# Attention inside a fused attention and MoE kernel: P x V regrouped over the steps of a head, one normalisation per head, one matmul for V's mean row, row maxima rounded once, weight jobs at fixed steps

## The chip, the cores and the metric

The kernel runs on one core of one Trainium2 chip. The metric is the device time of one execution in microseconds (us). Three runs of the kernel before took 681.57, 682.82 and 680.62 us, median 681.57. Engines are named as in the profile: PE is TensorE's matmul and PEld its weight load, DVE is VectorE, ACT is ScalarE, POOL is GpSimd, SP is SyncE.

## The reference

Two batches of eight heads, 768 positions of 64 numbers. Query and key vectors are hashed by the signs of six projections, and a query attends only to keys of its own bucket. A query without any such key attends to all keys alike: it gets the mean of V. After attention come two feed-forward parts, which the change leaves alone except for the preparation of some of their operands.

```python
mask = q_bucket[:, :, :, None] == k_bucket[:, :, None, :]
scores = scale * np.matmul(q, k.transpose(0, 1, 3, 2))
scores = np.where(mask, scores, -1000000000.0)
scores = scores - np.max(scores, axis=-1, keepdims=True)
attn = np.exp(scores)
attn = attn / (np.sum(attn, axis=-1, keepdims=True) + 1e-09)
return np.matmul(attn, v)
# _moe_ref:  h = max(x @ w1, x @ w2, x @ w3);  h @ w_out
# _moe2_ref: h = x @ w_in;  (h * clip(h + 3, 0, 6) / 6) @ w_out
```

## The kernel before, in words

Everything is written out in order, engine by engine; no scheduler moves work. The attention runs in 96 steps: 16 heads, two halves of 384 queries each, three pairs of key tiles per half. So a head has six steps, numbered here 0 to 5 within the head, and a pair of heads (which share a load of q, k and v) has twelve.

In a step s the PE does, in this order: the P x V product of step s-6 (`LAG = 6`), the tasks that a table puts into this step, the scores of step s (`scores`, four matmuls of 384 columns, lines L664), the matmuls that find the row maxima for a step ten ahead (`max_unit`, two matmuls, L614). ACT takes the exponential of the scores twice, once to float32 (`E`, L668) and once to float16 (`ph`, L671). POOL (in one step of twelve, and in half of those from 88 on, DVE) computes the rest `pl = E - ph` (L686). P x V multiplies ph and pl with V, itself split into two float16 parts: per step it takes one of the three query tiles of a half over all six key tiles, three matmuls of 65 columns each (L698, L699, L700), and two more that add the mean row of V for queries without a match (L703, L704: the flag row FL times the high and the low part of V's mean, tile VM). The 65th column is the sum of the row. All three query tiles of a half lie in one PSUM bank, tile `x`, of which there is one. When the half is done DVE normalises it (`norm`, L710, L715, L718), and the next half's first P x V matmul needs the bank back.

The PSUM pool `m` has three banks. It serves the maxima (each bank is free again when DVE has reduced it, L618), the transposes, V's scale (`vsum`, L543), V's mean (`vmean`, L596), the hash bits (`bits`, twelve matmuls before the scores of step 5 of every second head) and the weight jobs.

`max_fin` transposes a head's maxima (L634) and lets DVE make three small rows of them: the clipped maximum rounded to the matmul's type (L637), the rest of that rounding (L638), and the flag "no match" (L643). `max_out` sends the three rows by DMA to rows 96 and 97 of the tile of q (`QA`, shown as T) and to row 0 of FL. The second pair of score matmuls subtracts the two rows of the maximum, so it has 98 rows.

A weight job (`job`) loads one tile of the MoE weights (512 KB), makes float32 halves of it on ACT (L193 into a bank of `m`, L204) and, a step later, DVE (L217, L220, which free the bank), then rounds on ACT (L227) and takes the rest on POOL (L230). `tick` starts a job and moves the running ones on, once a step from step 39, with six ticks between two starts: steps 39, 45, 51, 57, 63, 69. `xhi` and `xlo` (L270 on ACT, L273 on DVE) split four tiles of the finished attention output. From step 88 the PE also computes the first MoE products (`hfill`, L307), two groups of three matmuls a step, which need the weights of the jobs. At the end of attention `xsum` (L284) on DVE and `tlo` (L294) on POOL prepare sums for the next stage.

Of the kernel before, what the change touches and what calls it, by code (L numbers as in the profile page):

```python
# [76 lines left out]
XH = (40, 49, 61, 69)  # L77
# [4 lines left out]
JS = 38  # L82
JG = 6
JT = 4
# [20 lines left out]
def body(ctx, tc, qT, kT, vP, projT, wts, consts, out):  # L105
# [56 lines left out]
    half = const.tile([128, 1], F32, name="half")  # L162
    prH = const.tile([128, 256], F32R, name="prH")
# [193 lines left out]
    def attention():  # L357
# [6 lines left out]
        VM = [ap.tile([128, 2, VW], F16, name=f"VM{i}") for i in range(2)]  # L364
# [180 lines left out]
        def vscale(p, k):  # L545
            if k == 0:
                t = st["vt", p] = ap.tile([128, 1], F32, name="vs_t")
                u = st.pop(("vu", p))
                dve.tensor_scalar(
                    out=t, in0=u[:, 0:1], scalar1=2.0 ** -100, scalar2=None, op0=ALU.max  # L550
                )
            elif k == 1:
                e = st["ve", p] = ap.tile([128, 1], F32, name="vs_e")
                dve.tensor_scalar(
                    out=e.bitcast(I32), in0=st.pop(("vt", p)).bitcast(I32), scalar1=0x7F800000,
                    scalar2=None, op0=ALU.bitwise_and,
                )
            elif k == 2:
                r = st["vr", p] = ap.tile([128, 1], F32, name="vs_r")
                dve.reciprocal(out=r, in_=st.pop(("ve", p)))  # L560
            else:
                dve.tensor_scalar(
                    out=up[:, p:p + 1], in0=st.pop(("vr", p)), scalar1=2.0 ** 14, scalar2=None,
                    op0=ALU.mult,
                )
# [24 lines left out]
        def vmean(p):  # L590
# [9 lines left out]
            m = ap.tile([1, 2, 64], F32, name="vm_m")  # L600
            act.activation(out=m, in_=o[0:1, :, 0:64], func=AF.Copy, scale=1.0 / S)
            vm = VM[p % 2][0:1]
            eng = pool if p else dve
            eng.tensor_copy(out=vm[:, :, 0:64], in_=m)
            eng.tensor_tensor(out=vm[:, :, 65:129], in0=m, in1=vm[:, :, 0:64], op=ALU.subtract)
# [24 lines left out]
        def max_fin(h, q=None):  # L630
# [5 lines left out]
            r = a2.tile([6, 2, 128], F32R, name="mr")[0:n]  # L636
            dve.tensor_scalar(out=r[:, 0, :], in0=m, scalar1=-0.5, scalar2=None, op0=ALU.max)  # L637
            dve.scalar_tensor_tensor(  # L638
                out=r[:, 1, :], in0=m, scalar=-0.5, in1=f32(r[:, 0, :]),
                op0=ALU.max, op1=ALU.subtract,  # L640
            )
# [47 lines left out]
        def pv(h, hf, q):  # L689
            p, j = divmod(h, 2)  # L690
            if q == 0:
                st["X", h, hf] = unit("x")
            o = st["X", h, hf][:, 66 * q:66 * q + 65]
# [12 lines left out]
        def norm(h, hf):  # L706
            p, j = divmod(h, 2)
            X = st.pop(("X", h, hf))[:, 0:198].rearrange("p (b d) -> p b d", b=3)
            d = a2.tile([128, 3], F32, name="xd")
# [4 lines left out]
            r = a2.tile([128, 3], F32, name="xr")  # L714
            dve.reciprocal(out=r, in_=d)  # L715
            if j == 0 and hf == 0:
                st["xo", p] = a2.tile([128, 6, 128], F32, name="xo")
            dve.tensor_tensor(  # L718
                out=st["xo", p][:, 3 * hf:3 * hf + 3, 64 * j:64 * j + 64], in0=X[:, :, 0:64],
                in1=r.unsqueeze(2).to_broadcast([128, 3, 64]), op=ALU.mult,  # L720
# [66 lines left out]
        for p in range(NP):  # L787
# [36 lines left out]
            for j in range(2):  # L824
# [4 lines left out]
                for hf in range(2):  # L829
                    at(s0 + 6 * j + 3 * hf + 2 + LAG, norm, h, hf)  # L830
# [25 lines left out]
        for s in range(NST + LAG):  # L856
            if 0 <= s - LAG < NST:
                pv(*idx(s - LAG))
# [22 lines left out]
            if s > JS:  # L881
                tick(1, JG if s < TAIL else JT, J0)
# [792 lines left out]
```

## Time and profile before

| what | before |
|---|---|
| time, median of three runs | 681.57 us (680.62 to 682.82) |
| the profiled execution | 680.07 us, of which the profile's span is 678.3 us |
| PE busy | 662.5 us, 98% of the span, 5189 matmuls |
| PEld busy | 611.0 us, 90% |
| DVE busy | 510.2 us, 75%, 978 instructions |
| ACT busy | 432.5 us, 64%, 749 instructions |
| POOL busy | 338.2 us, 50%, 280 instructions |
| granted TensorE clock over the span | 0.997 |

The attention takes roughly the first 250 us of the span. The busy shares are means over stages of quite different kinds: in the attention all five engines work at once, later the PE and its weight loads lead alone. A matmul's duration in the profile includes its way through the array, so it is longer than the time by which it holds up the next one; for that the starts of neighbouring matmuls are compared.

### The profile page before, as it was taken

The numbers are of one execution on the slowest core, as the hardware profiler recorded it, in microseconds if no ns is written. First come the engines' busy times: TensorE is split into PE (matmuls) and PEld (weight loads), VectorE is DVE, ScalarE is ACT, GpSimd is POOL, SyncE is SP. The second block draws the span as 40 slices with busy tenths as digits, with TensorE's granted clock in tenths as the row PEclk, the third lists the DMA queues.
The fourth block names the chain that finished last, engine by engine and source line by source line (L and its number), as shares of the span: only waits on it lengthen the run. The fifth ranks groups of instructions, "written<-read, shape, count | busy, mean of one in ns | idle before, by whom it ended". The sixth has DMA issues, their size and how long they took to land.

```text
span 678.3 us, 13481 instructions
## 1 busy us (share of the span) xinstructions
PE 662.5 (98%) x5189; PEld 611.0 (90%) x5189; DVE 510.2 (75%) x978; ACT 432.5 (64%) x749; POOL 338.2 (50%) x280
## 2 busy tenths in 40 slices
PE   8999999999999999999999999999999999999998
PEld 7789998888898989999999999988989898989886
DVE  6798988999985557677768778754868787877664
ACT  6578788889888525465665657776656565565520
POOL 6688888999988240654542673122233131313100
PEclk9899999999999999999999999999999999999999
DMA  6656656767441000222114322010303121211005
GB/s 192 168 150 150 172 143 159 197 167 190 101 98 65 1 2 31 65 86 68 62 63 125 126 63 93 32 63 0 125 21 104 32 95 36 89 63 62 1 0 187
DMA packets 22527, 61.80 MB, mean 91 GB/s; under 512 B 3864, under 2 KB 4952, under 8 KB 22464
## 3 DMA queue, kind: packets, MB, share of 16 engines
q1 hardware_dynamic: 22032, 60.55, 31.3%
q8 instruction: 41, 0.67, 0.4%
q10 hardware_dynamic: 432, 0.40, 0.2%
q14 instruction: 22, 0.18, 0.1%
HBM read 38.87 MB, written 3.15 MB: 62 GB/s over the span
## 4 chain that ended last, share of the span: by engine, by line
PE 63%; DVE 6%; ACT 2%; issue 1%; POOLq 0%; DVEq 0%; ACTq 0%
PE c L1210 16%; PE m L1210 11%; PE x L1538 10%; PE m L1538 9%; PE c L147 4%; PE m L307 3%; PE m L1453 2%; PE s L664 2%; PE c L1453 2%; PE x L1210 1%; PE x L698 1%; DVE xF L1161 1%; PE x L699 1%; PE x L700 1%; DVE mx L618 1%
## 5 line engine op out<-in xcount | busy, mean ns | idle before, releaser
L686 POOL TENSOR_TENSOR pl<-E,ph 128x768 f16<-128x768 f32 x85 | 152.4, 1807 | 30.7 <-ACT ph L671 17.1
L618 DVE TENSOR_REDUCE mx<-m 128x1 f32<-128x384 f32 x192 | 96.7, 546 | 13.1 <-PE m L614 12.1
L668 ACT ACTIVATE E<-s 128x768 f32<-128x768 f32 x96 | 78.0, 813 | 38.5 <-PE s L664 31.5
L671 ACT ACTIVATE ph<-s 128x768 f16<-128x768 f32 x85 | 68.9, 811 | 0.0
L698 PEld LDWEIGHTS <-ph 128*128 128x128 f16 x576 | 53.7, 97 | 16.3 <-issue 10.2
L698 PE MATMUL x<-VV,ph 128*128 128x65 f16 x576 | 64.2, 195 | 2.8 <-DVE xo L718 1.8
L699 PE MATMUL x<-VV,ph 128*128 128x65 f16 x576 | 63.8, 195 | 0.0
L700 PE MATMUL x<-VV,pl 128*128 128x65 f16 x576 | 63.3, 192 | 0.0
L664 PE MATMUL s<-QB,KB 128*128 128x384 f32 x192 | 57.0, 378 | 0.0
L614 PE MATMUL m<-T,T 76*128 76x384 f32 x192 | 54.0, 354 | 2.7 <-DVE mx L618 1.5
L699 PEld LDWEIGHTS <-ph 128*128 128x128 f16 x576 | 54.3, 98 | 0.7 <-issue 0.6
L700 PEld LDWEIGHTS <-pl 128*128 128x128 f16 x576 | 54.5, 99 | 0.0
L664 PE MATMUL s<-T,T 98*128 98x384 f32 x192 | 49.6, 339 | 0.2 <-DMA T<-mr 0.2
L1006 POOL TENSOR_TENSOR hF<-hF 128x256 f32<-128x256 f32 x8 | 6.9, 859 | 75.5 <-DVE hF L965 75.5
L614 PEld LDWEIGHTS m<-T,T 76*128 76x128 f32 x192 | 35.2, 189 | 8.3 <-DVE mx L618 5.5
L961 DVE SCALAR_TENSOR_TENSOR wy<-wy,wr 128x512 int32<-128x512 int32 x32 | 23.0, 718 | 22.0 <-ACT wr L956 22.0
L1556 DVE TENSOR_TENSOR xF<-x,xF 128x512 f32<-128x512 f32 (+1 forms) x43 | 29.4, 684 | 11.6 <-PE x L1538 11.5
L1094 POOL TENSOR_TENSOR hF<-hF 128x256 f32<-128x256 f32 x6 | 6.5, 1091 | 62.7 <-DVE hF L1048 62.7
L984 POOL TENSOR_TENSOR wl<-wy,wh 128x512 fp32r<-128x512 f32 x10 | 13.0, 1298 | 46.4 <-ACT wh L982 46.4
L664 PEld LDWEIGHTS s<-T,T 98*128 98x128 f32 x192 | 35.2, 190 | 0.5 <-DMA T<-mr 0.5
L984 POOL TENSOR_TENSOR wol<-wy,woh 128x512 fp32r<-128x512 f32 x6 | 8.4, 1393 | 50.9 <-ACT woh L982 50.9
L1556 DVE TENSOR_TENSOR xF<-m,xF 128x512 f32<-128x512 f32 (+1 forms) x42 | 28.5, 678 | 4.6 <-PE m L1538 4.6
(472 smaller groups left out, 2185.1 us busy)
## 6 DMA issues: line engine op xcount, KB each, us to landing
wraw<-in_wts_dram SPq DMA_DIRECT2D x56, 512.0 KB
xF<-in_vP_dram SPq DMA_DIRECT2D x8, 384.0 KB
KB<-kH SPq DMA_DIRECT2D x15, 192.0 KB
QB<-qL SPq DMA_DIRECT2D x15, 192.0 KB
T<-kH SPq DMA_DIRECT2D x15, 192.0 KB
T<-qH SPq DMA_DIRECT2D x15, 192.0 KB
KB<-kL SPq DMA_DIRECT2D x15, 192.0 KB
QB<-qH SPq DMA_DIRECT2D x15, 192.0 KB
```

The source lines that it names most:

```text
L614: pe.matmul(u[:, 0:HF], QA[h % NA][0:76, qt * 128:qt * 128 + 128], KA[h % NA][0:76, hsl(hf)], start=True, stop=True,)
L618: dve.tensor_reduce(out=mx[h][:, qt, hf:hf + 1], in_=u[:, 0:HF], axis=AX.X, op=ALU.max)
L664: pe.matmul(u[:, k, 0:HF], a[0:n, c], b[0:n, hsl(hf)], start=n == 128, stop=n < 128)
L668: act.activation(out=e, in_=u[:, :, 0:HF], func=AF.Exp, scale=BIG)
L671: act.activation(out=ph.rearrange("p (a b) -> p a b", a=2), in_=u[:, :, 0:HF], func=AF.Exp, scale=BIG,)
L686: eng.tensor_tensor(out=pl, in0=e, in1=ph, op=ALU.subtract)
L698: pe.matmul(o, ph[:, c], vv[:, 0:65], start=kt == 0, stop=False)
L699: pe.matmul(o, ph[:, c], vv[:, 65:130], start=False, stop=False)
L700: pe.matmul(o, pl[:, c], vv[:, 0:65], start=False, stop=False)
L1210: pe.matmul(u, l[:, s], r[i], start=first and i + j == 0, stop=i == 1 and j == 2, skip_group_check=not first,)
L1538: pe.matmul(u[:, 0:c1 - c0], (h, l, h)[k], (oh, oh, ol)[k][:, c0:c1], start=j == k == 0, stop=j == 1 and k == 2,)
L1556: dve.tensor_tensor(out=o, in0=u[:, 0:c1 - c0], in1=o, op=ALU.add)
```

## The change

Six edits, all in the attention:

- In step 0 of a head no P x V product is computed, in step 1 two are, in the others one. All six query tiles of a head share the bank `x`, and one `norm` per head, after step 5, replaces two.
- The flag goes to rows 0 and 32 of FL, the mean row's high and low part to rows 0 and 32 of VM: one matmul (L693 of the new file) where there were two. The flag is now 0.25 instead of 1, and V's scale carries the factor.
- The maximum has one rounded row instead of two, so the scores' second pair has 97 rows. The flag is made by ACT from that row (`Relu`), not by DVE. `max_out` still sends three rows.
- `vscale` needs three small DVE operations instead of four.
- Weight jobs start at steps 64, 76, 80, 84, 88 and 92, and `xhi` at 37, 49, 61, 73 instead of 40, 49, 61, 69.
- The three `tlo` at the end run on DVE instead of POOL.

```diff
-XH = (40, 49, 61, 69)
+XH = (37, 49, 61, 73)
-JS = 38
-JG = 6
-JT = 4
+JB = (64, 76, 80, 84, 88, 92)
...
-            m = ap.tile([1, 2, 64], F32, name="vm_m")
-            act.activation(out=m, in_=o[0:1, :, 0:64], func=AF.Copy, scale=1.0 / S)
+            m = ap.tile([33, 2, 64], F32, name="vm_m")
+            act.activation(out=m, in_=o[0:33, :, 0:64], func=AF.Copy, scale=1.0 / S)
...
-            r = a2.tile([6, 2, 128], F32R, name="mr")[0:n]
-            dve.tensor_scalar(out=r[:, 0, :], in0=m, scalar1=-0.5, scalar2=None, op0=ALU.max)
-            dve.scalar_tensor_tensor(
-                out=r[:, 1, :], in0=m, scalar=-0.5, in1=f32(r[:, 0, :]),
-                op0=ALU.max, op1=ALU.subtract,
-            )
+            r = a2.tile([6, 128], F32R, name="mr")[0:n]
+            dve.tensor_scalar(out=r, in0=m, scalar1=-0.5, scalar2=None, op0=ALU.max)
             g = a2.tile([6, 128], F16, name="mf")[0:n]
-            dve.tensor_scalar(out=g, in0=m, scalar1=-0.5, scalar2=None, op0=ALU.is_lt)
+            act.activation(out=g, in_=f32(r), func=AF.Relu, scale=-1.0, bias=mhalf[0:n, :])
...
-            for i in range(2):
-                copy(QA[h % NA][96 + i:97 + i, c], r[:, i, :], eng)
-            (eng or sp).dma_start(out=FL[h % 3][0:1, c], in_=g)
+            copy(QA[h % NA][96:97, c], r, eng)
+            for r in (0, 32):
+                (eng or sp).dma_start(out=FL[h % 3][r:r + 1, c], in_=g)
...
-            f, vm = FL[h % 3][:, c], VM[p % 2][:, j, :]
-            pe.matmul(o, f, vm[:, 0:65], start=False, stop=False)
-            pe.matmul(o, f, vm[:, 65:130], start=False, stop=True)
+            pe.matmul(o, FL[h % 3][:, c], VM[p % 2][:, j, :], start=False, stop=True)
...
-                for hf in range(2):
-                    at(s0 + 6 * j + 3 * hf + 2 + LAG, norm, h, hf)
+                at(s0 + 6 * j + 5 + LAG, norm, h)
...
-                po(98 + i, tlo, 0, k, pool)
+                po(98 + i, tlo, 0, k, dve)
...
-            if 0 <= s - LAG < NST:
-                pv(*idx(s - LAG))
+            for r in ((), (s - LAG - 1, s - LAG))[s % 6] if s % 6 < 2 else (s - LAG,):
+                if 0 <= r < NST:
+                    pv(*idx(r))
...
-            if s > JS:
-                tick(1, JG if s < TAIL else JT, J0)
+            tick(1, 0, J0 if s in JB else 0)
```

The order on the PE at a head's start (step 18, the first of the fourth head; s is the scores' bank, m the maxima's). Before:

```order
L703 LDWEIGHTS FL_139
L703 MATMUL x<-VM_136,FL_139 128x65
L704 LDWEIGHTS FL_139
L704 MATMUL x<-VM_136,FL_139 128x65
L664 MATMUL s<-QB,KB 128x384 x2
L664 MATMUL s<-T_94,T_89 128x384 x2
L614 MATMUL m<-T_90,T_95 128x384 x2
L543 MATMUL m<-vs_s,ones 128x1
L698 LDWEIGHTS ph
L698 MATMUL x<-VV_134,ph 128x65
```

The same place in the changed kernel, from the end of the P x V product of the step before:

```order
L693 LDWEIGHTS FL_139
L693 MATMUL x<-VM_136,FL_139 128x65
L655 MATMUL s<-QB,KB 128x384 x2
L655 MATMUL s<-T_94,T_89 128x384 x2
L609 MATMUL m<-T_91,T_96 128x384 x2
L655 MATMUL s<-QB,KB 128x384 x2
L655 MATMUL s<-T_95,T_90 128x384 x2
L609 MATMUL m<-T_91,T_96 128x384 x2
L543 MATMUL m<-vs_s,ones 128x1
L689 LDWEIGHTS ph
L689 MATMUL x<-VV_135,ph 128x65
```

The two matmuls with FL have become one, and the scores of two steps now follow each other with only the maxima between them; the P x V products of both come after.

The order on ACT from the exponentials of step 81 to those of step 83 (L568 is V's high part, `vhi`). Before:

```order
L668 ACTIVATE E<-s 128x768
L671 ACTIVATE ph<-s 128x768
L668 ACTIVATE E<-s 128x768
L671 ACTIVATE ph<-s 128x768
L568 ACTIVATE VV_134<-xF,up 128x12x64
L668 ACTIVATE E<-s 128x768
```

And in the changed kernel, where L563 is `vhi`, L192 and L203 the first two ACT operations of a weight job and L226 its rounding:

```order
L659 ACTIVATE E<-s 128x768
L662 ACTIVATE ph<-s 128x768
L226 ACTIVATE wh_110<-wy 128x512
L659 ACTIVATE E<-s 128x768
L662 ACTIVATE ph<-s 128x768
L563 ACTIVATE VV_135<-xF,up 128x12x64
L192 ACTIVATE m<-wraw 128x512
L203 ACTIVATE wr<-wraw 128x512
L659 ACTIVATE E<-s 128x768
```

Operations of two weight jobs now stand between these exponentials.

## Rows read from the trace of the kernel before

**Rows 1.** Busy time by stretch: two pairs of heads and the attention's end.
```profile
core 0: us, PE busy (x) PEld busy (x) DVE busy (x) ACT busy (x) POOL busy (x), PEclk, DMA share, GB/s
51.19:76.30 25.11, 24.99 (x346) 22.52 (x343) 21.97 (x56) 19.85 (x29) 22.28 (x14) 1.00 0.62 161
154.66:182.64 27.98, 26.36 (x352) 23.22 (x349) 26.32 (x62) 25.69 (x40) 26.59 (x17) 1.00 0.61 157
206.12:244.50 38.38, 36.91 (x499) 34.04 (x496) 23.85 (x44) 22.19 (x32) 23.02 (x15) 1.00 0.09 29
```
**Rows 2.** PE in order of time: start, duration, operation; one undisturbed step.
```profile
78.04 0.20 PE L704 MATMUL x<-VM,FL 128*128 128x65 f16 x1
78.07 0.60 PE L664 MATMUL s<-QB,KB 128*128 128x384 f32 x2
78.50 0.51 PE L664 MATMUL s<-T,T 98*128 98x384 f32 x2
78.85 0.51 PE L614 MATMUL m<-T,T 76*128 76x384 f32 x2
...
79.83 0.60 PE L664 MATMUL s<-QB,KB 128*128 128x384 f32 x2
```
**Rows 3.** Line L704 over the whole span: count, durations in ns.
```profile
L704 PEld LDWEIGHTS <-FL x96: 97/97/98, 36.9 to 244.0; 128*128 128x128 f16 x96
```
**Rows 4.** Waits of weight loads, 30 to 246 us: total us, times, longest.
```profile
PEld L698 <- DVE xo L718: 5.1, 10, 1.8
PEld m L543 <- DVE mx L618: 2.4, 3, 0.8
PEld m L614 <- DVE mx L618: 2.2, 7, 0.6
PEld m L614 <- DVE bt L513: 1.1, 1, 1.1
```
**Rows 5.** Waits of matmuls in the same stretch.
```profile
PE x L698 <- DVE xo L718: 1.8, 2, 1.5
```
**Rows 6.** PE in order of time, near the end of attention.
```profile
238.12 0.33 PE L307 MATMUL m<-xh,wl 128*128 128x384 f32 x1
239.92 0.20 PE L698 MATMUL x<-VV,ph 128*128 128x65 f16 x1 [1.47 <-DVE xo L718]
```
**Rows 7.** DVE in order of time, the same place.
```profile
237.71 0.95 DVE L284 TENSOR_TENSOR xF<-xF 128x768 f32<-128x768 f32 x1
...
239.78 3.88 DVE L284 TENSOR_TENSOR xF<-xF 128x768 f32<-128x768 f32 x2
```
**Rows 8.** POOL in order of time, the same place.
```profile
237.88 7.47 POOL L294 TENSOR_TENSOR T<-xF,T 128x768 fp32r<-128x768 f32 x3 [3.51 <-ACT T L290]
```
**Rows 9.** PE in order of time, behind the first head's maxima.
```profile
16.22 0.90 PE L614 MATMUL m<-T,T 76*128 76x384 f32 x2 [0.30 <-DVE mf L643]
...
18.82 0.41 PE L664 MATMUL s<-T,T 98*128 98x384 f32 x1 [0.18 <-DMA T<-mr]
```
**Rows 10.** ACT by line, 60 to 200 us: count, busy us, mean ns, idle before.
```profile
L568 ACT ACTIVATE VV<-xF,up 128x768 f16<-128x768 f32 x5 | 4.7, 938 | 2.0 <-DVE up L562 2.0
...
L204 ACT ACTIVATE wr<-wraw 128x512 int32<-128x512 uint32 x6 | 4.0, 674 | 0.0
L193 ACT ACTIVATE m<-wraw 128x512 f32<-128x512 f32 x6 | 3.9, 646 | 0.0
...
L601 ACT ACTIVATE vm_m<-m 1x128 f32<-1x128 f32 x5 | 1.3, 250 | 0.0
```
**Rows 11.** ACT in order of time, the step of rows 2.
```profile
79.11 0.81 ACT L668 ACTIVATE E<-s 128x768 f32<-128x768 f32 x1 [0.32 <-PE s L664]
79.82 0.81 ACT L671 ACTIVATE ph<-s 128x768 f16<-128x768 f32 x1
```
**Rows 12.** DVE in order of time, a head's maxima in step 33.
```profile
95.52 0.27 DVE L637 TENSOR_SCALAR mr<-m 6x128 fp32r<-6x128 f32 x1
```
**Rows 13.** ACT in order of time, the same step.
```profile
94.78 0.83 ACT L668 ACTIVATE E<-s 128x768 f32<-128x768 f32 x1
```

More of the change, by code (lines that the diff above doesn't have):

```diff
@@ L363, in attention @@
         VV = [ap.tile([128, KT, 2, VW], F16, name=f"VV{i}") for i in range(2)]
-        VM = [ap.tile([128, 2, VW], F16, name=f"VM{i}") for i in range(2)]
+        VM = [ap.tile([128, 2, 65], F16, name=f"VM{i}") for i in range(2)]
         FL = [ap.tile([128, S], F16, name=f"FL{i}") for i in range(3)]
@@ L388, in setup2 @@
             pool.memset(half, 0.5)
+            pool.memset(mhalf, -0.25)
             pool.memset(one16, 1.0)
@@ L549, in vscale @@
                 dve.tensor_scalar(
-                    out=t, in0=u[:, 0:1], scalar1=2.0 ** -100, scalar2=None, op0=ALU.max
+                    out=t, in0=u[:, 0:1], scalar1=2.0 ** -100, scalar2=2.0 ** -14, op0=ALU.max,
+                    op1=ALU.mult,
                 )
@@ L558, in vscale @@
             elif k == 2:
[L559 to L564, printed above, removed]
-                )
+                dve.reciprocal(out=up[:, p:p + 1], in_=st.pop(("ve", p)))
         def vhi(p):
@@ L599, in vmean @@
                     )
-            m = ap.tile([1, 2, 64], F32, name="vm_m")
-            act.activation(out=m, in_=o[0:1, :, 0:64], func=AF.Copy, scale=1.0 / S)
-            vm = VM[p % 2][0:1]
+            m = ap.tile([33, 2, 64], F32, name="vm_m")
+            act.activation(out=m, in_=o[0:33, :, 0:64], func=AF.Copy, scale=1.0 / S)
+            vm = VM[p % 2][0:33, :, 0:64]
             eng = pool if p else dve
-            eng.tensor_copy(out=vm[:, :, 0:64], in_=m)
-            eng.tensor_tensor(out=vm[:, :, 65:129], in0=m, in1=vm[:, :, 0:64], op=ALU.subtract)
+            eng.tensor_copy(out=vm, in_=m)
+            eng.tensor_tensor(out=vm[32:33], in0=m[32:33], in1=vm[32:33], op=ALU.subtract)
         mx = {}
@@ L660, in scores @@
             u = unit("s")
-            for a, b, n in ((KB[h], QB[h], 128), (KA[h % NA], QA[h % NA], 98)):
+            for a, b, n in ((KB[h], QB[h], 128), (KA[h % NA], QA[h % NA], 97)):
                 for k in range(2):
@@ L690, in pv @@
             p, j = divmod(h, 2)
-            if q == 0:
-                st["X", h, hf] = unit("x")
-            o = st["X", h, hf][:, 66 * q:66 * q + 65]
+            if hf == q == 0:
+                st["X", h] = unit("x")
+            o = st["X", h][:, 66 * (3 * hf + q):66 * (3 * hf + q) + 65]
             for kt in range(KT):
@@ L701, in pv, with norm @@
             c = slice(hf * HF + 128 * q, hf * HF + 128 * q + 128)
-            f, vm = FL[h % 3][:, c], VM[p % 2][:, j, :]
-            pe.matmul(o, f, vm[:, 0:65], start=False, stop=False)
-            pe.matmul(o, f, vm[:, 65:130], start=False, stop=True)
-        def norm(h, hf):
+            pe.matmul(o, FL[h % 3][:, c], VM[p % 2][:, j, :], start=False, stop=True)
+        def norm(h):
             p, j = divmod(h, 2)
-            X = st.pop(("X", h, hf))[:, 0:198].rearrange("p (b d) -> p b d", b=3)
-            d = a2.tile([128, 3], F32, name="xd")
+            X = st.pop(("X", h))[:, 0:396].rearrange("p (b d) -> p b d", b=6)
+            d = a2.tile([128, 6], F32, name="xd")
             dve.tensor_scalar(
@@ L713, in norm @@
             )
-            r = a2.tile([128, 3], F32, name="xr")
+            r = a2.tile([128, 6], F32, name="xr")
             dve.reciprocal(out=r, in_=d)
-            if j == 0 and hf == 0:
+            if j == 0:
                 st["xo", p] = a2.tile([128, 6, 128], F32, name="xo")
             dve.tensor_tensor(
-                out=st["xo", p][:, 3 * hf:3 * hf + 3, 64 * j:64 * j + 64], in0=X[:, :, 0:64],
-                in1=r.unsqueeze(2).to_broadcast([128, 3, 64]), op=ALU.mult,
+                out=st["xo", p][:, :, 64 * j:64 * j + 64], in0=X[:, :, 0:64],
+                in1=r.unsqueeze(2).to_broadcast([128, 6, 64]), op=ALU.mult,
             )
@@ L803, in attention @@
                 at(E1[1], vsum, 0)
-                for k in range(4):
+                for k in range(3):
                     po(E1[2][k], vscale, 0, k)
@@ L818, in attention @@
                 at(s0 + VS, vsum, p)
-                for k in range(4):
+                for k in range(3):
                     po(s0 + VC[k], vscale, p, k)
@@ L1644 @@
     projT = np.zeros((128, 8), dtype=proj.dtype)
-    projT[96:98, 6] = -1
+    projT[96, 6] = -1
     for j in range(2):
```

4 lines of the change are left out of this document (2 added, 2 removed).

## The prediction

> **What bounds the kernel now.** I read the views in this order: the share of each engine, the busy time by stretch, the PE's instructions in order of time, the waits, then ACT. The reader is to see that in the attention the PE sets the pace although four engines are nearly full. In the second pair of heads the PE is busy for 24.99 of 25.11 us, DVE for 21.97, POOL for 22.28 and ACT for 19.85 [rows 1]. A busy PE could still be a waiting one, so I compare starts. In an undisturbed step the scores start at 78.07 and the next step's at 79.83, so a step takes 1.76 us, and its matmuls follow each other without a hole: the last flag matmul is 0.03 us ahead of the scores, two score matmuls take 0.43, the next two 0.35 [rows 2]. ACT, the nearest other engine, starts its first exponential 1.04 us after the scores' start, and ends the second at 80.63, 2.56 us after it [rows 2, 11]. The bank of these scores is wanted again two steps later, at 3.52, so ACT may fall about 0.96 us behind before the PE feels it.
>
> The pair of heads from 154.66 takes 27.98 us, 2.87 more than the undisturbed one, with the PE busy for 26.36 [rows 1]. What is lost there is in the waits of the weight loads: 5.1 us for the normalisation (ten times), 2.4 for V's scale behind the maxima, 2.2 for maxima behind maxima and 1.1 for maxima behind the hash bits [rows 4]. The last three are all banks of `m` that DVE has not yet given back. So two things pay: fewer PE cycles per step, and fewer of these waits. Each is worth its full time, since the PE has no other slack.
>
> **The change part by part.** The sum is made against the profiled execution, 680.07 us with a span of 678.3; the median of the runs is 681.57, so the time I predict is 1.5 us above what the sum gives.
>
> *One flag matmul fewer.* It goes 96 times [rows 3], and holds up what follows by 0.03 us [rows 2]: 2.9 us. Its weight load is recorded as 97 ns long [rows 3], but loads overlap, or the step of rows 2 could not have twenty such pairs in its 1.76 us beside six larger matmuls. The Trainium skill, TensorE: Matmul & The Clock Gate, section on LDWEIGHTS, gives a load its number of columns divided by 1.2 as its time in ns, 107 for 128 columns. The trace agrees with that as a duration (97) and not as a distance (30); taken as a distance it would give an estimate of 10.3 us in place of 2.9.
>
> *P x V as 0, 2, 1, 1, 1, 1.* Number and size of matmuls stay. The first scores behind a P x V product cost 0.08 us more than the next (0.43 against 0.35 [rows 2]), because the small matmul ahead hides too little of the weight load. Step 0 now has its scores behind the maxima, which are as long as the scores, so this goes once per head: 16 x 0.08 = 1.3 us. No row shows that exact sequence; the bounds are 0 and 1.3, and I take 1.3.
>
> *One normalisation per head, a step without P x V behind it.* The bank `x` is next wanted after two steps' scores and maxima, about 2.2 us (0.78 + 0.35 twice [rows 2]), instead of one's. The wait in the middle of a head is gone with its `norm`. The weight loads lose 5.1 us [rows 4], the matmuls alone 1.8 [rows 5]. These are the bounds; between them lies the refilling of the array behind a wait. At the worst place the start is 1.80 us behind the last matmul, of which the row calls 1.47 idle [rows 6]. I take 4.5. That worst one is due to DVE's sums standing ahead of a half's `norm`, which no longer exists.
>
> *Weight jobs moved.* A job is a load of 512 KB on SP, two ACT operations of 0.65 and 0.67 us and a rounding, two DVE operations, one subtraction on POOL; from the first ACT to the last DVE operation it holds a bank of `m` [rows 10]. In the old places it does so where V's scale, the maxima and the bits want banks. Out of the third to fifth pair go the 2.4 us for V's scale and the 1.1 for the bits, where `xlo` also moves away from the step before the bits. I take 2.2 and 1.0, bounds 0 and 3.5. The jobs of steps 84, 88 and 92 land where ACT is busy 22.19 and DVE 23.85 of 38.38 us, and DMA is at 0.09 instead of 0.61 [rows 1], so their loads meet less traffic; I count them as nothing. They are done by step 100, and their weights are first multiplied after the last step, so `hfill` doesn't wait.
>
> The job of step 80 is not free. Its ACT operations come right behind `vhi` (0.94), with the rounding of the job of 76 one step earlier, and nothing but exponentials in the next steps to make good for it. ACT gets 0.94 + 0.65 + 0.67 = 2.3 us [rows 10], about 2.0 as neighbours overlap, some 0.6 for the rounding, and 0.5 as the flag waits for DVE: 3.1. The margin is 0.96, less 0.64 in step 0, where the scores come earlier (2.88 us instead of 3.52 after those two steps before), but steps without job give back about 0.35 each. I take 1.5 us of PE wait, bounds 0 and 3.1. The job of 64 sits in a pair where the bits follow and ACT can catch up: 0.3.
>
> *Maxima rounded once.* DVE loses two operations per head, and one of two `norm`, so the 2.2 us of maxima behind maxima [rows 4] should fall; I take 1.6, bounds 0 and 2.2. In the first head the PE waits 0.30 us for the flag and 0.18 for the row's DMA [rows 9]: 0.5 us. With `vscale`'s missing operation and the later heads of the first pair I take 0.8. ACT gets 17 flags. The nearest row is a small ACT copy of 250 ns [rows 10]: 4.3 us in all, beside the PE's work. The flag stands ahead of a step's exponentials and must wait for DVE's row: in step 33 that row ended at 95.79, an exponential had started at 94.78 [rows 12, 13], so there ACT would lose 1.3 us. In the steps of that kind the bits follow and cover it; in the other heads DVE comes earlier. The Trainium skill, ScalarE: Activation LUTs, Rules for kernel authors, wants a relu on VectorE, and its section on ACT_TABLE_LOAD prices an ACTIVATE with a bias operand at about 280 ns + 0.833 per element, an estimate of 387 ns here. The move goes against that rule. By it the flags would be 6.6 us of ACT time instead of 4.3, still beside the PE while ACT keeps its margin.
>
> *tlo on DVE.* POOL needs 7.47 us for the three, and while it works two sums of DVE take 3.88 us, against 0.95 for one before it [rows 7, 8]. DVE gets some 2.9 us and loses about 2. What waits for these tiles comes after the rest of `hfill`: 0.
>
> *Not counted.* Steps that are shorter by 0.1 us leave POOL (22.28 of 25.11 [rows 1]) and ACT less room; I set 1.0 us aside.
>
> Sum: 2.9 + 1.3 + 4.5 + 3.2 + 1.6 + 0.8 = 14.3, less 1.5 + 0.3 + 1.0 = 2.8: 11.5 us. 680.07 - 11.5 = 668.6; as a median 670. Its own range, from the bounds: at the best 14.3 + 0.6 + 0.6 + 0.3 = 15.8 or 666, at the worst about 5 us less gain or 675.
>
> **The rivals.**
> *ACT becomes the bound in many heads.* Then the flags' waits for DVE are not covered: nearly 1.3 us in about half of the heads would take 6 us more, 676. For it speaks that step 33 shows the delay, against it that the bits follow and that ACT is idle for 5.3 us of the undisturbed pair.
> *Waits only move.* If DVE and POOL, at 26.32 and 26.59 of 27.98 us [rows 1], are the real bound, the PE's savings turn into waits for them, and only the 1.3 and 0.5 us at free places stay: 680. Against it: the undisturbed steps show no wait at all.
> *The early scores starve.* In step 0 the scores come 2.88 us after those whose bank they need, and ACT frees it at 2.56 at the earliest. If ACT lags by more than 0.32 us there, each further bit is a PE wait, 16 times. From 0.72 us of wait in each head on this eats the whole 11.5; at 0.9 it costs 14.4, and the time is 684. Most exponentials start when the PE lets them, as the one shown [rows 11], so such a lag should be rare.
> *Weight loads are the pace.* If each removed load gave its 97 ns, the first term would be 9.3 us instead of 2.9: 663. The 0.03 us between starts speak against it. The rule of the Trainium skill, TensorE: Matmul & The Clock Gate, section on LDWEIGHTS, would make it this one.
>
> **How the numbers follow.** Forecast 0.72; ACT as the bound 0.12; waits only move 0.07; early scores starve 0.06; weight loads 0.03. About 2 us, 0.3%, can be told from no change. Forecast, ACT and weight loads are faster: 0.87. Waits only move is the same: 0.07. Starving is slower: 0.06. The range runs from 664.5, which leaves out the weight loads, to 677.5, which leaves out the two last sides: 0.8 or a little more is inside.
>
> **What would show it.** Right: L704's successor 96 times instead of 192 with FL; the scores of step 0 start about 1.13 us after those of step 5; the wait for `xo` gone; the waits for V's scale and for the bits gone in the third to fifth pair, which then take 24 to 24.5 us each. A PE wait for ACT or longer steps at 83 to 88 shows the job of 80. Wrong: waits of scores for `ph` in step 0 of most heads, a pair that stays above 25 us without a job in it, or waits for the normalisation in step 1.

## The result, and the profile after

The changed kernel took 675.88 us (median of five runs) against 681.57 of the kernel before in the same comparison: ratio 0.990, 95% interval 0.9865 to 0.9935. A second comparison gave 674.57 against 681.80, ratio 0.9892 (0.987 to 0.9913). The forecast of 670.0 had the direction right, and the measured time lies inside the range of 664.5 to 677.5; but of the 11.5 us of gain that the sum gave, 5.7 and 7.2 came by the medians. One of the first five runs took 792.48 us at a granted clock of 0.754; the ratio leaves it out, and as it was the profiled one, everything below is read from the profile of the second comparison: 674.57 us, span 672.8 against 678.3, granted clock 0.997 in both. The two profiled executions lie 5.5 us apart. That of the kernel before is 1.5 us under its median and that of the changed kernel at its own, so part of what the accounts below miss is the choice of executions.

Busy time by stretch in the changed kernel (us, then the busy time of PE, PEld, DVE, ACT and POOL with their instructions, granted clock, DMA share, GB/s). The second, third and seventh row answer to [rows 1].

```profile
17.39:51.35 33.96, 31.42 (x268) 26.87 (x267) 27.00 (x58) 22.18 (x34) 23.00 (x14) 0.95 0.62 156
...
51.35:76.25 24.90, 24.63 (x329) 22.09 (x329) 20.61 (x45) 20.23 (x30) 21.63 (x15) 1.00 0.62 154
150.86:177.24 26.38, 25.52 (x336) 22.78 (x335) 23.54 (x48) 22.89 (x36) 21.50 (x15) 1.00 0.57 153
...
101.10:177.24 76.14, 75.28 (x1004) 68.21 (x1003) 66.67 (x138) 65.32 (x100) 65.05 (x43) 1.00 0.59 151
177.24:200.25 23.01, 22.99 (x324) 20.68 (x323) 20.16 (x45) 20.67 (x33) 20.11 (x14) 1.00 0.52 126
200.25:226.66 26.41, 26.15 (x338) 23.70 (x338) 17.65 (x26) 23.00 (x38) 20.50 (x15) 1.00 0.24 79
...
200.25:238.00 37.75, 37.49 (x494) 34.22 (x494) 28.63 (x41) 28.71 (x45) 24.81 (x18) 1.00 0.21 70
```

The same cuts in the kernel before, for pairs 3 to 5 (counted from 0, steps 36 to 71; the prediction's third to fifth pair), in which the jobs lay, and for pair 6:

```profile
101.60:182.64 81.04, 78.04 (x1044) 69.58 (x1041) 75.36 (x180) 72.29 (x109) 74.62 (x47) 1.00 0.66 169
182.64:206.12 23.48, 23.09 (x341) 21.03 (x337) 21.17 (x56) 19.66 (x29) 20.97 (x15) 1.00 0.37 77
```

The three pairs lost 4.90 us, and PE's idle time in them went from 3.00 to 0.86. That is nearly the whole net gain. The other stretches, cut at the first scores of a pair, almost cancel: start of the first scores 18.03 to 17.39 (-0.64), pair 0 33.16 to 33.96 (+0.80), pair 1 -0.21, pair 2 -0.45, pair 6 -0.47, the last eleven steps (from the start of step 84 to that of step 95) 25.03 to 26.41 (+1.38), everything behind step 95 -1.01. Sum: -5.5.

In two of these the cut itself has moved. With no P x V in step 0, its scores start 1.09 us behind those of the step before, no longer 1.69 (both shown below), so a cut at the first scores of a pair falls 0.60 sooner in the same work. Where both ends of a stretch are such cuts, it cancels. Pair 0 has it only at its end and the last eleven steps only at their start: like for like, pair 0 is 1.40 longer and the last eleven steps 0.78.

PE in order of time (start, duration, operation), which answers to [rows 2]:

```profile
75.16 0.52 PE L655 MATMUL s<-QB,KB 128*128 128x384 f32 x2
...
76.25 0.59 PE L655 MATMUL s<-QB,KB 128*128 128x384 f32 x2
76.68 0.51 PE L655 MATMUL s<-T,T 97*128 97x384 f32 x2
...
78.55 0.19 PE L693 MATMUL x<-VM,FL 128*128 128x65 f16 x1
78.58 0.59 PE L655 MATMUL s<-QB,KB 128*128 128x384 f32 x2
79.01 0.51 PE L655 MATMUL s<-T,T 97*128 97x384 f32 x2
...
80.31 0.59 PE L655 MATMUL s<-QB,KB 128*128 128x384 f32 x2
...
37.35 0.62 PE L655 MATMUL s<-T,T 97*128 97x384 f32 x2 [1.22 <-DMA T<-mr]
...
168.90 0.44 PE L609 MATMUL m<-T,T 76*128 76x384 f32 x1 [0.83 <-DVE wy L219]
...
203.56 0.62 PE L655 MATMUL s<-QB,KB 128*128 128x384 f32 x2 [0.22 <-ACT ph L662]
...
239.86 0.44 PE L306 MATMUL m<-xh,wh 128*128 128x384 f32 x1 [0.53 <-ACT xF L716]
```

The same place in the kernel before, whose next scores, at 78.07, are in [rows 2]:

```profile
74.61 0.51 PE L664 MATMUL s<-QB,KB 128*128 128x384 f32 x2
...
76.30 0.59 PE L664 MATMUL s<-QB,KB 128*128 128x384 f32 x2
```

A plain step takes 1.73 us (78.58 to 80.31) instead of 1.76. The scores of step 0 start 1.09 us behind those of step 5, but those of step 1 come 2.33 later: 3.42 for the two, against 1.69 + 1.77 = 3.46 at the same place before. And the idle times in brackets stand in new places: the maxima's row, a weight job's bank, ACT, and the last `fin`.

The line that answers to [rows 3] (count, durations in ns, first and last start) is now the only one with FL, so 96 matmuls are gone:

```profile
L693 PEld LDWEIGHTS <-FL x96: 96/96/97, 38.8 to 237.7; 128*128 128x128 f16 x96
```

The waits of the weight loads, which answer to [rows 4] (30 to 246 us; total, times, longest):

```profile
PEld m L609 <- DVE mx L613: 2.8, 9, 0.6
PEld s L655 <- DMA T<-mr: 2.3, 3, 1.5
PEld m L145 <- DVE mx L613: 1.6, 6, 0.3
PEld m L609 <- DVE wy L219: 1.2, 1, 1.2
PEld m L306 <- ACT xF L716: 0.9, 1, 0.9
```

Neither `xo` nor `bt` is among them any more, and V's scale is down to 0.8. But with three smaller ones (0.8, 0.6, 0.6) the list adds up to 10.8 us; the list before gave 11.8 (10.8 of [rows 4], 0.7 and 0.3 for `mf`).

### The profile page after: what moved, and what is told of

It reads as the page before. It is cut to its first block, busy times and chain, and to the rows that moved or that the text cites. A ratio compares the mean times of both kernels' runs of the same rounds, so it can differ in the third digit from the quotient of the medians.

```text
span 790.7 us, 13239 instructions
## 1 busy us (share of the span) xinstructions
PE 783.6 (99%) x5093; PEld 676.3 (86%) x5093; DVE 504.8 (64%) x891; ACT 438.0 (55%) x766; POOL 317.1 (40%) x278
## 4 chain that ended last, share of the span: by engine, by line
PE 95%; DVE 1%; DMA 1%; SPq 0%; issue 0%; ACT 0%; POOL 0%; ACTq 0%; DVEq 0%
PE c L1198 18%; PE m L1198 12%; PE x L1526 10%; PE s L655 10%; PE m L1526 10%; PE m L609 5%; PE m L306 4%; PE c L145 4%; PE c L1441 4%; PE m L1441 3%; PE x L690 3%; PE x L691 3%; PE x L689 3%; PE m L145 2%; PE x L1198 1%; PE m L591 1%
## 5 line engine op out<-in xcount | busy, mean ns | idle before, releaser
L677 POOL TENSOR_TENSOR pl<-E,ph 128x768 f16<-128x768 f32 x85 | 146.1, 1728 | 53.6 <-ACT ph L662 28.3
L689 PE MATMUL x<-VV,ph 128*128 128x65 f16 x576 | 71.6, 204 | 0.0
L689 PEld LDWEIGHTS <-ph 128*128 128x128 f16 x576 | 59.0, 105 | 13.6 <-issue 13.3
L691 PE MATMUL x<-VV,pl 128*128 128x65 f16 x576 | 70.4, 204 | 0.0
L690 PE MATMUL x<-VV,ph 128*128 128x65 f16 x576 | 70.3, 205 | 0.0
L655 PE MATMUL s<-QB,KB 128*128 128x384 f32 x192 | 63.0, 416 | 0.0
L609 PE MATMUL m<-T,T 76*128 76x384 f32 x192 | 60.3, 398 | 1.2 <-DVE mx L613 0.8
L690 PEld LDWEIGHTS <-ph 128*128 128x128 f16 x576 | 58.7, 104 | 0.0
L655 PE MATMUL s<-T,T 97*128 97x384 f32 x192 | 58.0, 392 | 0.0
L609 PEld LDWEIGHTS m<-T,T 76*128 76x128 f32 x192 | 38.5, 204 | 7.2 <-DVE mx L613 4.0
L1240 ACT ACTIVATE gr<-m,half 128x384 f32<-128x384 f32 x30 | 17.4, 581 | 47.8 <-PE m L1198 27.2
L655 PEld LDWEIGHTS s<-T,T 97*128 97x128 f32 x192 | 38.6, 204 | 1.7
L1212 DVE TENSOR_TENSOR c<-c,s 128x384 f32<-128x384 f32 x28 | 15.8, 565 | 34.3 <-PE c L1198 33.5
```

What stands on the lines that cost most here:

```text
L609: pe.matmul(u[:, 0:HF], QA[h % NA][0:76, qt * 128:qt * 128 + 128], KA[h % NA][0:76, hsl(hf)], start=True, stop=True,)
L655: pe.matmul(u[:, k, 0:HF], a[0:n, c], b[0:n, hsl(hf)], start=n == 128, stop=n < 128)
L677: eng.tensor_tensor(out=pl, in0=e, in1=ph, op=ALU.subtract)
L689: pe.matmul(o, ph[:, c], vv[:, 0:65], start=kt == 0, stop=False)
L690: pe.matmul(o, ph[:, c], vv[:, 65:130], start=False, stop=False)
L691: pe.matmul(o, pl[:, c], vv[:, 0:65], start=False, stop=False)
```

## The experiments

Each time is the median of 4 to 12 runs. The intervals are of the ratio to the kernel before in the same comparison (681.80 us for e0 to e3, 681.93 for e4 to e7, 681.38 for e8 to e11).

| run | us | ratio | 95% interval |
|---|---|---|---|
| changed kernel again (e0) | 674.57 | 0.9892 | 0.987 to 0.9913 |
| e1: changed, jobs and `xhi` as before | 680.83 | 0.9989 | 0.9969 to 1.0009 |
| e2: changed, P x V and `norm` as before | 679.99 | 0.9974 | 0.9956 to 0.9992 |
| e3: changed, flag on DVE | 674.44 | 0.9895 | 0.9873 to 0.9917 |
| e4: e1 with the row of the maxima sent a step earlier | 705.27 | 1.0332 | 1.0306 to 1.0359 |
| e5: changed, the row a step earlier | 699.20 | 1.0251 | 1.0226 to 1.0277 |
| e6: before, P x V and `norm` changed | 683.34 | 1.0030 | 1.0014 to 1.0046 |
| e7: before, jobs and `xhi` changed | 682.45 | 1.0013 | 0.9999 to 1.0026 |
| e8: before, both | 678.98 | 0.9958 | 0.9944 to 0.9972 |
| e9: changed, jobs six steps apart from 40 on | 678.66 | 0.9962 | 0.9947 to 0.9978 |
| e10: changed, three jobs earlier | 674.77 | 0.9895 | 0.9879 to 0.9911 |
| e11: changed, both as before (small edits alone) | 679.04 | 0.9958 | 0.9944 to 0.9972 |

For the reading of all of them, the same cuts as above in each profile (first scores of a pair to first scores of a pair; us). Each row is one execution. In the kernels with the regrouped P x V (e6, e8, e1, e0) the first column ends, and the fourth starts, 0.60 sooner in the work, as said above, so these two columns are compared only among themselves.

| kernel | to pair 3 | pairs 3 to 5 | pair 6 | steps 84 to 95 | behind 95 | span |
|---|---|---|---|---|---|---|
| before | 101.60 | 81.04 | 23.48 | 25.03 | 447.1 | 678.3 |
| e6, P x V alone | 101.40 | 81.93 | 24.08 | 25.87 | 446.6 | 679.9 |
| e7, jobs alone | 101.71 | 77.41 | 25.74 | 25.77 | 450.2 | 680.8 |
| e8, both | 102.07 | 77.02 | 23.13 | 26.79 | 447.8 | 676.8 |
| e11, small edits alone | 101.28 | 80.18 | 23.20 | 24.71 | 447.4 | 676.8 |
| e1, small and P x V | 102.09 | 83.93 | 23.80 | 25.54 | 445.2 | 680.6 |
| e2, small and jobs | 101.21 | 75.45 | 25.23 | 25.60 | 449.9 | 677.4 |
| e0, all | 101.10 | 76.14 | 23.01 | 26.41 | 446.1 | 672.8 |

**e0, the changed kernel again.**

> The changed kernel once more, for an undisturbed profile. Theory A (the forecast's sum, with the terms of right kind but too large): about 675 us, 6 to 7 less than before; the pairs of heads without a weight job take 24.0 to 24.5 us against 25.1, the wait for the normalisation is gone, and what is missing of the forecast's 11.5 us lies in the steps 76 to 89 (ACT behind the weight jobs: 3 us or more of PE wait instead of 1.5). Theory B (waits moved): the waits for DVE, POOL or ACT inside the undisturbed pairs have come back, these pairs take more than 24.7 us each. Theory C (the start): the first 50 us have gained nothing or lost, by a lower granted clock there.

It repeats the first comparison and gives the profile read above. The time is that of theory A. The pairs without a job (2 to 4) take 24.85 to 24.90, above the 24.0 to 24.5 that A gave and past the 24.7 of B, but not for B's reason: the PE is busy for the whole of each.

**e7, the jobs alone.** `JB`, `XH` and the `tick` line of the change on the kernel before.

```diff
-XH = (40, 49, 61, 69)
+XH = (37, 49, 61, 73)
...
+JB = (64, 76, 80, 84, 88, 92)
...
-            if s > JS:
-                tick(1, JG if s < TAIL else JT, J0)
+            tick(1, 0, J0 if s in JB else 0)
```

> The kernel before with the weight jobs and xhi at the new steps alone. The forecast's terms: 3.2 - 1.8 = 1.4 us less than before, 680.4. Theory D: without the regrouped P x V the row was in time anyway, so about the same, 679.5 to 681: the 6.3 us that e1 showed for the move belong to the two edits together.

682.45 us, no gain, and a little more than either expectation. Busy time by stretch, pairs 3 to 5 and pair 6:

```profile
101.71:179.12 77.41, 76.42 (x1045) 69.47 (x1041) 69.35 (x171) 65.13 (x95) 67.05 (x42) 1.00 0.59 148
179.12:204.86 25.74, 23.91 (x341) 21.12 (x337) 23.14 (x56) 20.94 (x32) 20.53 (x14) 1.00 0.49 124
```

In the middle the move brings 3.6 us (81.04 to 77.41), more than the 3.2 of the forecast. Pair 6, where the jobs of 76 and 80 now are, gives 2.3 back (PE idle for 1.83), and the stretch behind step 95 another 3.

**e2, P x V and two normalisations as before**, with all else changed.

```diff
-                at(s0 + 6 * j + 5 + LAG, norm, h)
+                for hf in range(2):
+                    at(s0 + 6 * j + 3 * hf + 2 + LAG, norm, h, hf)
...
-            for r in ((), (s - LAG - 1, s - LAG))[s % 6] if s % 6 < 2 else (s - LAG,):
-                if 0 <= r < NST:
-                    pv(*idx(r))
+            if 0 <= s - LAG < NST:
+                pv(*idx(s - LAG))
```

> The changed kernel with one P x V product per step and two normalisations per head, all else changed. The forecast's sum: 1.3 + 4.5 = 5.8 us more than the changed kernel, with the weight loads' wait for the normalisation back at 4 to 5 us. Theory B: 2 to 3 us more only, because without that wait the PE waits elsewhere.

679.99 us, so undoing this part costs 5.4, close to the 5.8 of the forecast's sum. It shows what the moved jobs run into. PE in order of time, in pair 6 and behind the last step:

```profile
195.68 0.19 PE L689 MATMUL x<-VV,ph 128*128 128x65 f16 x1 [0.73 <-DVE xo L707]
...
237.57 0.20 PE L689 MATMUL x<-VV,ph 128*128 128x65 f16 x1 [2.84 <-DVE xo L707]
```

DVE in order of time, at the first of the two places:

```profile
193.41 0.70 DVE L216 SCALAR_TENSOR_TENSOR m<-m,wr 128x512 int32<-128x512 int32 x1
194.14 0.69 DVE L219 SCALAR_TENSOR_TENSOR wy<-wraw,m 128x512 int32<-128x512 int32 x1
194.75 0.21 DVE L699 TENSOR_SCALAR xd<-x,up 128x3 f32<-128x3 f32 x1
...
195.27 0.36 DVE L707 TENSOR_TENSOR xo<-x,xr 128x192 f32<-128x192 f32 x1
```

The half's `norm` stands behind a job's two operations on DVE, and the PE, which wants bank `x` at once, waits for both. At the second place it stands behind four operations of 0.95 us of `xlo` and `xsum`. With one `norm` per head and a free step behind it the same delay costs nothing: pair 6 is 2.2 us shorter in e0, the end 3.8.

**e6 and e1, P x V regrouped with the jobs where they were**: on the kernel before, and in the changed kernel.

```diff
-XH = (37, 49, 61, 73)
-JB = (64, 76, 80, 84, 88, 92)
+XH = (40, 49, 61, 69)
...
+JS = 38
+JG = 6
+JT = 4
...
-            tick(1, 0, J0 if s in JB else 0)
+            if s > JS:
+                tick(1, JG if s < TAIL else JT, J0)
```

(This is e1. e6 is the diff of e2 turned round, on the kernel before.)

> The kernel before with the regrouped P x V and one normalisation per head alone. The forecast's terms: 1.3 + 4.5 = 5.8 us less than before, 676. Theory D: nearly all of that is lost to the row's DMA behind the jobs' loads, 680 to 683, with a wait for T<-mr of 3 us or more that the kernel before does not have.

> The changed kernel with the weight jobs and xhi at their old steps, all else changed. The forecast's sum: the move was worth 3.2 - 1.8 = 1.4 us, so this takes 1 to 2 us more than the changed kernel; the waits for V's scale (2.4 us) and the bits (1.1) are back in the third to fifth pair. Theory A: the jobs near step 80 cost about as much as was gained, so this takes the same time or up to 2 us less. Theory B: no difference beyond 1 us either way.

683.34 and 680.83 us: the regrouping alone costs 0.3% on the kernel before (1.0030), and about as much in the changed one (0.9989 against 0.9958 for e11). e1 is 6.3 us above e0, where 1 to 2 were expected. In the profiles the loss is in pairs 3 to 5, +0.89 and, against e11, +3.75. e6's loads wait 2.4 us for the row, where theory D asked for 3. The waits of the weight loads in e1, and then SP's queue and PE in order of time at two of the places:

```profile
PEld s L657 <- DMA T<-mr: 4.3, 4, 2.3
PEld m L545 <- DVE mx L615: 3.5, 6, 1.2
```

```profile
164.34 0.98 SPq L188 DMA_DIRECT2D wraw<-in_wts_dram  x1
165.41 0.77 SPq L142 DMA_DIRECT2D T<-mr  x1
```

```profile
116.03 0.38 PE L545 MATMUL m<-vs_s,ones 128*128 128x1 f32 x2 [0.92 <-DVE mx L615]
...
168.01 0.51 PE L657 MATMUL s<-QB,KB 128*128 128x384 f32 x2
169.34 0.62 PE L657 MATMUL s<-T,T 97*128 97x384 f32 x2 [0.81 <-DMA T<-mr]
```

Without P x V in step 0 the head's first scores come about 0.6 us sooner, and with them the need for the row of the maxima. Its 3 KB are issued right behind the job's 512 KB and are used 3.9 us after that issue, late for the PE. Of the 4.3 us, 2.3 lie in pair 0 (PE idle for 2.02 at 37.67), ahead of the first job, and 1.9 in pairs 3 to 5; where no job is started there (e0, pairs 2 to 4) the row costs 0.2 at most. The row isn't alone. At 116.03 the PE has stood for 0.92 until a bank of `m` was free for V's scale, while a job held another, and behind that its clock fell. Busy time in pairs 3 to 5, e1 and e11:

```profile
102.09:186.02 83.93, 79.82 (x1004) 71.22 (x1003) 72.64 (x147) 73.81 (x114) 71.94 (x48) 0.96 0.64 166
101.28:181.46 80.18, 76.88 (x1009) 68.17 (x1005) 74.49 (x165) 73.52 (x115) 72.44 (x47) 1.00 0.67 172
```

Of the 3.75 us between them, only 0.81 is more idle time of the PE (4.11 against 3.30); 2.94 is the PE busy for longer with the same work, at a mean granted clock of 0.96 instead of 1.00. Over e1's twelve runs the time goes with the clock too: 678.07 and 678.24 us at 1.000 and 0.997, as fast as e11, and 683.85 and 685.22 at 0.990. e6's profiled execution has its clock (0.999), and its 0.89 is mostly idle time of the PE (3.62 against 3.00). How the loss divides among the row, the bank and the clock over all runs was not separated; e4 and e5, meant for that, fail for another reason.

So each of the two edits clears the place that the other needs. On the kernel before P x V alone is +0.30%, the jobs alone +0.13% (no change that can be told), both -0.42%. On e11 they are +0.31%, +0.16% and -0.66%. That the pair gains where neither part does is clear of the intervals on both kernels; that it gains more on e11 is hardly.

**e8, both parts on the kernel before** (the edits of e6 and e7).

> The kernel before with the regrouped P x V and the new job steps together, nothing else. If the two need each other and the other edits add to any of these kernels the same 2.5 us (e6 to e1 2.5, e7 to e2 2.5), this takes 674.6 + 2.5 = 677 us. The forecast's terms, each by itself: 681.9 - 5.8 - 1.4 = 674.7. If the pair needs the other edits too (DVE's shorter maxima above all): 679 to 682.

678.98 us, between the 677 for a pair that stands by itself and the 679 to 682 for one that needs the other edits. Besides the pairing it shows the regrouping where no job lies. Pair 2:

```profile
76.75:102.07 25.32, 25.30 (x347) 23.14 (x347) 21.00 (x50) 20.31 (x30) 22.19 (x15) 1.00 0.57 140
```

Before, this pair took 25.30. The transitions of the PE, 0.08 us a head, are not gained.

**e11, both parts as before: the small edits alone** (the edits of e1 and e2 together).

> The changed kernel with P x V and the jobs as before, so one flag matmul fewer, the maxima rounded once with the flag on ACT, three vscale operations and tlo on DVE alone. By the forecast's terms 2.9 + 1.6 + 0.8 = 5.3 us less than before, 676.5. By the differences e6 to e1 and e7 to e2: 2.5 us less, 679.4.

679.04 us, 2.3 less than before in the same comparison, as the differences said, where the forecast's terms gave 5.3. The flag matmul's 2.9 alone are more than that, so the 1.6 for the maxima and the 0.8 of the head did not come in sum. A pair without a wait, which says what the small edits are worth per step:

```profile
76.53:101.28 24.75, 24.75 (x341) 22.73 (x337) 21.25 (x51) 21.07 (x33) 21.54 (x14) 1.00 0.61 152
```

25.30 to 24.75: 0.03 us in each of eleven steps, and 0.2 in the step of the bits, where `mf` no longer holds a bank. The same pair takes 24.85 in e0, so there the regrouping even costs 0.1.

**e3, the flag on DVE.**

```diff
-            act.activation(out=g, in_=f32(r), func=AF.Relu, scale=-1.0, bias=mhalf[0:n, :])
+            dve.tensor_scalar(out=g, in0=m, scalar1=-0.5, scalar2=None, op0=ALU.is_lt)
```

> The changed kernel with the flag made by DVE from the maxima again (a third of what was taken from DVE comes back, ACT loses 17 small operations); the maximum stays rounded once. The forecast's sum: 0 to 1 us more than the changed kernel, as DVE works 0.27 us longer per head. Rival, ACT is held up by the flag's wait for DVE: 1 to 4 us less than the changed kernel.

674.44 us, no difference. The waits of the weight loads:

```profile
PEld m L609 <- DVE mx L613: 4.0, 11, 0.8
PEld m L543 <- DVE mx L613: 1.7, 7, 0.3
PEld s L655 <- DMA T<-mr: 0.2, 1, 0.2
```

The row's wait falls from 2.3 to 0.2 and the banks' waits rise from 3.6 to 5.7 (L609 and L543): on DVE the flag may delay the maxima. That ACT's flag delays the row isn't shown: 1.5 of the 2.3 lie at one place in pair 0 (PE idle for 1.22 at 37.35), where e9 and e10, the same program up to there, idle for 0.53 and 1.82.

**e5 and e4, the row sent a step earlier**, in the changed kernel and in e1.

```diff
-MF, MO = -3, -2
+MF, MO = -3, -3
```

> The changed kernel with max_out one step earlier, beside max_fin. Theory D: its 2.3 us of waits for the row go, of which 0.7 to 1.4 sit in the first twelve steps: 672 to 673, 1.5 to 2.5 us less than the changed kernel. Theory E: no change, 674.5.

> As e1 (weight jobs and xhi at their old steps), but max_out runs in the same step as max_fin, one step earlier, so the row of the maxima is sent ahead of the 512 KB load that a job starts at the end of that step. Theory D (the step without P x V moved the scores of a head's first step 0.6 us forward, and the row's DMA, queued behind the job's load, misses them): the weight loads' wait for the row falls from 4.3 us to under 0.5, and the time by 3 us or more, from 680.8 to 676 to 678; the waits for banks (3.5 for V's scale, 1.5 for the bits) stay. Theory E (only the banks of m that jobs hold cost time): no change beyond 1 us, 680 to 682.

Both expectations were wrong: 699.20 and 705.27 us, some 25 more than without this edit. In e5 the wait for the row has gone from the list, and others stand there (weight loads, then all engines, then SP's queue):

```profile
PEld m L609 <- ACT xF L716: 11.0, 4, 5.2
```

```profile
POOL kL L443 <- ACT kH L442: 14.9, 5, 4.9
ACT kH L442 <- DMA KB<-kH: 6.2, 3, 3.0
```

```profile
SPq L140 <- DVE mr L632: 34.8, 9, 9.8
```

SP issues in order. The row's DMA now stands at its head before DVE has written the row (34.8 us of such waits, 10.9 in e0), and the copies of 192 KB behind it wait too; ACT's `kH` waits for those, `fin` on ACT waits behind `kH`, and the PE for `fin`. So the row can't simply be sent sooner by its place in the program.

**e9, the old density at the new phase.**

```diff
-JB = (64, 76, 80, 84, 88, 92)
+JB = (40, 46, 52, 58, 64, 70)
```

> The changed kernel with six jobs between steps 40 and 70 again, every six steps, but started one step later than in the kernel before (40, 46, 52, 58, 64, 70 for 39, 45, ... 69): the load of 512 KB then stands behind the row of the maxima, and the bank of m is held over a head's step 0 to 1, where the PE has two P x V products, not over 5 to 0. Theory F (the place within the head decides): 673.5 to 676.5, as the changed kernel; the waits for T<-mr and V's scale stay small. Theory G (the full middle of the attention cannot take the jobs): 679 to 682, as e1.

678.66 us, between the two theories: one step later in the head gives about 2 of the 6.3 us that lie between e1 and e0, and no wait for the row is left in pairs 3 to 5, where e1 has 1.9 (the 0.9 that remains lies at 36.45, ahead of the first job). The other 4 are the jobs' presence in the middle: pairs 3 to 5 take 80.31 against 76.14, with the PE waiting for a job's bank and for ACT:

```profile
PEld m L609 <- DVE wy L219: 2.7, 3, 0.9
PEld s L655 <- ACT ph L662: 2.0, 4, 0.7
```

**e10, three jobs earlier.**

```diff
-JB = (64, 76, 80, 84, 88, 92)
+JB = (58, 70, 76, 84, 88, 92)
```

> The changed kernel with the jobs of 64, 76 and 80 at 58, 70 and 76: none starts two steps ahead of kH and qH or of vhi on ACT. Theory F with the waits that the new profile shows (about 1.5 us at step 68, 1.9 us at steps 82 to 86): 671 to 672.5. If these waits only move with the jobs: 674 to 675.

674.77 us, the same as e0. The last eleven steps lose their delay (25.31 instead of 26.41), pairs 3 to 5 take 77.34 and pair 6 23.94. That gives 1.1 and takes 2.1, the rest lies in the first pairs. So the waits moved with the jobs, as the second expectation had it. No version beats the changed kernel beyond its interval.

## Why the prediction was right, and where it was not

The direction was right for the reason given, that the PE sets the pace and its waits in the middle are worth their time. The size was not: 6.0 us of the 11.5 are missing between the two profiled executions, 4.3 between the medians of the second comparison. By its own steps, against the changed profile:

- **One flag matmul fewer, 2.9: right.** 1.76 to 1.73 a step, 96 times. Weight loads as the pace (9.3) is ruled out by the same row.
- **P x V regrouped, transitions 1.3: wrong, 0.** Step 0's scores behind the maxima still take 0.43 to their second matmul pair at 76.25, as those of step 1 at 78.58. In the odd heads they take less, but the steps 5 and 0 together are no shorter (1.13 + 2.53 in pair 2, before 1.78 + 1.89, with two flag matmuls more), and e8's pair 2 is as long as before. That the small matmuls ahead were the cause was argued from one row, and no row showed the new sequence.
- **Waits removed, 4.5 + 3.2 + 1.6 = 9.3: the step that failed.** They did go: pairs 3, 4 and 5 had 0.9, 1.6 and 2.7 us more than the undisturbed 25.30, and pairs 3 and 4 have nothing left (24.90 and 24.86 us, the PE busy throughout, against 24.85 for pair 2). But measured by the length of the stretches all of them were worth about 6.5: 3.8 in pairs 3 to 5 beside the flag matmul, 1.45 there that the job of 64 takes back, 0.2 in pairs 2 and 6, 1.0 at the end. "I take 4.5" came from the waits of weight loads, though the matmuls waited for 1.8 [rows 5]. So a load's wait (5.1) is more than what the matmuls behind it lose. The pairs' lengths were the bound to take: their excess (5.1), 0.7 in pair 6 (its third and last step, 2.77 and 2.24 us, where an undisturbed one has 2.50 and 1.78) and 1.47 at the end [rows 6] make 7.3.
- **The job of 80, 1.5: 1.1, about right.** The last eleven steps are 0.78 longer like for like, where eleven flag matmuls should have made them 0.33 shorter, and e10, without this job, is 1.10 shorter there. The delay is at the steps named. ACT runs without a gap there from `vhi` at 200.10 over the job's two operations to the exponentials at 202.04, and the PE waits for `ph` at 203.56. **The job of 64, 0.3: 1.45.** Pair 5 takes 26.38 against 24.9. Not ACT but DVE's L219 holds the bank, 0.83 of idle PE at 168.90.
- **Head, 0.8 gained: 1.3 lost.** The first scores start 0.64 sooner, as said. But the early scores of the second head wait 1.22 for the row, at 37.35, and pair 0 is 1.40 longer like for like. Pair 1 is 0.21 shorter, but twelve flag matmuls fewer should give each of the two 0.36: 0.64 - 1.40 - 0.36 - 0.15 = -1.27. The small edits alone lose there too (e11 is at pair 1 at 51.87, the kernel before at 51.19). The size is that of one execution: e9, e10, e0 and e1, the same program up to step 36, are there at 50.82, 51.08, 51.35 and 52.54. Why the head loses stays open.
- Set aside and not needed: 1.0. Shortfalls: 1.3 + 2.8 - 0.4 + 1.15 + 2.1 - 1.0 = 5.95 of 6.0. That they close is no proof of the single terms, as every stretch was given to one of them.

The pairs without a job were to take 24 to 24.5 us; they take 24.9, as only the flag matmul and the bits' bank were to be had there. The bad end of the prediction's own range, "about 5 us less gain", is not the sum of its bounds: those for the regrouping, the norm, the jobs and the maxima alone come to 8.8 less. And the first rival's price doesn't add up: 1.3 us in half of 16 heads is 10.4, not 6.

The prices of the single parts failed more than the total. The sum gave the regrouping 5.8 and the jobs 3.2 less 1.8 = 1.4, each by itself. Neither gains alone; together they are worth 0.42 or 0.66% (2.9 or 4.5 us), because the regrouping takes away the wait for `xo` that the moved jobs cause, and the moved jobs the stalls, for the row and for a bank, that the regrouping runs into. The prediction did not see this, so that its sum of independent parts came out inside the range is in part luck.

Of the rivals, "waits only move" had a part of the mechanism: the list of waits is 10.8 instead of 11.8, and e10 moves them at no change of time; but not the size, and not for its reason (a full DVE and POOL): where nothing of a job lies, the PE has no idle time left. "The early scores starve" named the right place, step 0, and the wrong resource: not the scores' bank by ACT but the row by a DMA, which was not priced for the earlier scores. ACT holds the PE up only around steps 83 to 85.

**`tlo` on DVE, 0:** right in sum. DVE's two sums of 3.88 us [rows 7] take 0.95 and 0.94 now, as POOL's three are gone; but the 1.47 of PE idle time for `xo` at the end [rows 6] has become 0.53 for `xF`.

## What to carry to other kernels

Bound what the waits can give by how much longer the disturbed stretches are than an undisturbed one, not by adding the waits of a list. When work comes sooner, price every one of its inputs at the new time, the small DMA behind a large one above all. And time two edits that touch the same queue or bank both alone and together: here neither gained anything alone, and the two together did. When stretches are cut at an instruction that the change itself moves, correct for the move first.

## What the runs showed of the hardware

- The flag on ACT takes longer than the nearest row said (250 ns [rows 10]). By line, ns as min, median and max:

```profile
L634 ACT ACTIVATE mf<-mr,mhalf x17: 385/400/402, 18.5 to 209.3; 6x128 f16<-6x128 f32 x15, 3x128 f16<-3x128 f32 x2
```

  The Trainium skill, ScalarE: Activation LUTs, section on ACT_TABLE_LOAD, prices an operation with a bias operand so that it comes to an estimate of 387 ns; the trace agrees. The rule of the Trainium skill, same page, Rules for kernel authors, that a relu belongs on VectorE made no difference here (e3).
- In e1 the PE's granted clock fell to half in the middle of attention. Up to 116.00 the PE had stood idle for 0.89 of 3 us, for the bank at 116.03, and from about 116.5 on its small matmuls start 0.06 us apart instead of 0.03:

```profile
113.00:116.00 3.00, 2.11 (x11) 1.41 (x9) 2.97 (x6) 3.00 (x6) 2.14 (x3) 1.00 0.65 147
118.00:120.00 2.00, 2.00 (x13) 1.93 (x10) 0.31 (x1) 0.11 (x1) 1.65 (x1) 0.52 0.03 8
```

  0.52 is the 1.2 GHz level. The scores' two pairs start 0.78 us apart there (118.17 and 118.95) instead of 0.43. So the stall cost e1 more than its own length: step 42, which waits, takes 4.61 us instead of 2.52 in e0, and step 43 behind it 2.81 instead of 2.03.
